# Batch 1's queries transposed by DMA, three parameter rows spread by TensorE, and batch 1's values loaded between the halves of W2

## The chip, the cores and the metric

One NeuronCore of a Trainium2 chip runs the whole kernel. Its engines are TensorE (PE, matrix products into PSUM; PEld is its loading of weights), VectorE (DVE), ScalarE (ACT) and GpSimd (POOL); SyncE (SP) and POOL issue the DMAs used here. SP's go to a hardware queue and POOL's to a software queue, which also converts types on the way. The metric is the device time of one execution in microseconds, from the first instruction to the end of the program, as a median of several runs.

## The reference

Four batches go through sorted attention and then through a residual MLP. Cut to what matters:

```python
for _ in range(5):                         # sort_net -> P, rows and columns normalised
    P = softmax-like row and column scaling
k_sorted = einsum('bhij,bhjcd->bhicd', P, k_blocks)   # 8 blocks of 96 positions
v_sorted = einsum('bhij,bhjcd->bhicd', P, v_blocks)
attn = softmax(q_block @ k_sorted_block.T / sqrt(64)) # block by block
x = (attn @ v_sorted_block)                           # -> [4, 768, 512]

a1 = alpha1 * x + beta1
u = x + lam * einsum('ts,bsd->btd', w_tok, a1)
a2 = alpha2 * u + beta2
out = u + lam * (relu(a2 @ w_ch1) @ w_ch2)            # 512 -> 2048 -> 512
```

q, k and v are [4, 8 heads, 768, 64], all inputs float32; the output is [4, 768, 512] float32. The kernel computes in float16 and bfloat16 with float32 sums.

## The kernel before

**Stages.** Batch 0's attention comes first, while weights load. Then TensorE goes through the batches in halves of 384 positions. For each batch b and half hf there is an "h" stage of 16 units (`h_unit`, lines 770 and 1088: 512 to 2048 with a ReLU on ACT) and a "c" stage, the product with W2. For batch 0 the c stage has three tiles of 128 positions (`ch_unit`, line 773), each in four parts, and after each part a slot "c", 0 to 11. Later batches use `ch_pair` instead.

**An order written out by hand.** Every engine works through its own list in program order; an instruction that waits holds back all behind it on that engine, and this goes for SP's and POOL's DMA issues too. `put(b, hf, kind, n, f)` (line 993) hangs a piece of work behind unit n of a stage, and `run` emits it there. So the attention of batch 1 is spread over the stages (0,0) and (0,1) of batch 0, and so on.

**Batch 1's attention.** It needs, in this order:

- k and v in `raw` tiles (`load_kv`, line 195, two POOL DMAs each) and q in `qn` (`load_q`, line 185). For batch 1 q comes in contiguous slabs (`load_slabs`), for later batches in position order, six POOL DMAs. The tag "qn" has one buffer, the tag "raw" two.
- `mix_v` (line 552): TensorE mixes the blocks of v by the sorting matrix, ACT copies the result to `mixed`; three parts. `bounce_v` writes `mixed` to DRAM in two DMAs and `back_v` (line 593) reads it back into `Vs` with positions on partitions, on SP, in one DMA.
- `mix_k` (line 567): three parts; TensorE mixes and turns the keys, ACT writes `kT` in four copies per part.
- q turned to `qT`. For batch 1, `q_turn_late` (line 538) does this four times by 24 small TensorE products with an identity and two VectorE copies; for later batches `q_cross` (line 531) does it with a transposing DMA on SP for each 128 positions.
- `score` (line 414): TensorE, then ACT's exponential; the first is at (0,1,"h",0), the next at 1 and 2. One score covers two heads and half of the positions, that is 384 columns of `qT`. `pv` (line 490) uses `Vs` from unit 3 on.

**Other work on the same queues.** `moe_cross(0, 1)` (line 732) turns u of batch 0's second half with three transposing DMAs on SP into `uT`, from which VectorE makes `a2T`, the input of stage (0,1) "h". The finished tiles `ost` are stored by SP (line 788). `loads(2)` (line 545), at slot c 11, has POOL copy one element of `Vs` first, so that the loads of batch 2 start when `Vs` is back.

**Parameters.** alpha1, beta1 and lam are loaded spread over 128 partitions by three POOL DMAs (lines 947 to 949) into `alphaB`, `betaB` (float16) and `lamB`. `scale_affine` (line 630) multiplies the first two by 64 lam on VectorE between the `first_finish` steps of batch 0, and `scale_weights` (line 793) makes `lam16` from `lamB` and scales W2p with it. `brow` holds beta1 * lam in single rows.

**Loads on POOL's queue**, in order: q, v, k of batch 0, w_tok, the three parameters, W1 in four pieces, W2 in four pieces, v, k and q of batch 1.

**PSUM.** Tag psA has two tiles of two banks each (`psa`), psB four tiles of one bank (`psb`). A tile's next user waits until the last one's reader is through.

Of the kernel before, what the change touches and what calls it, by code (L numbers as in the profile page):

```python
# [7 lines left out]
FT = mybir.dt.float32  # L8
F16 = mybir.dt.float16
BF = mybir.dt.bfloat16  # L10
AF = mybir.ActivationFunctionType
# [5 lines left out]
def kernel(  # L17
# [75 lines left out]
    def const(shape, dtype, name):  # L93
        return wts.tile(shape, dtype, name=name, tag=name)
# [11 lines left out]
    bet1 = att.tile([1, C], FT, name="bet1", tag="ost", bufs=4)  # L106
    nc.sync.dma_start(lam1[:], moe_lam.rearrange("(o c) -> o c", o=1))
    nc.sync.dma_start(bet1[:], moe_beta1.rearrange("(o c) -> o c", o=1))

    KT0 = att.tile([128, H4, NB, 128], F16, name="kT0", tag="tw", bufs=2)  # L110
    VD = att.tile([128, D, 64], F16, name="vd", tag="tw", bufs=2)
# [5 lines left out]
    def load_slabs(dst, src):  # L117
        flat = src.rearrange("h s d -> (h s d)").rearrange("(g p f) -> p g f", p=128, f=12 * D)
        for g in range(0, H4, 2):
            pool.dma_start(dst[:, g:g + 2, :], flat[:, g:g + 2, :])  # L120
# [54 lines left out]
    W2p = const([128, HT, C], F16, "W2p")  # L175
    w1v = moe_w_ch1.rearrange("(ci p) n -> p ci n", p=128)
    w2v = moe_w_ch2.rearrange("(m p) c -> p m c", p=128)
    alphaB = const([128, C], F16, "alphaB")
    betaB = const([128, C], F16, "betaB")
    lamB = att.tile([128, C], FT, name="lamB", tag="kT", bufs=1)  # L180
    vscr = dram.tile([B, H * NB, BLK, D], F16, name="vscr", tag="vscr")
    raw_of = {}
    qn_of = {}

    def load_q(b):
        if b == 1:
            qn_of[b] = att.tile([128, H4, 12 * D], F16, name="q8b", tag="qn", bufs=1)
            return load_slabs(qn_of[b], q[b])
        qn_of[b] = att.tile([128, NT, H, D], F16, name="qn", tag="qn", bufs=1)
        for kt in range(NT):  # L190
            pool.dma_start(
                qn_of[b][:, kt, :, :], q[b, :, kt * 128:(kt + 1) * 128, :].rearrange("h p d -> p h d"),
            )

    def load_kv(b):
        for kv, src in ((1, v), (0, k)):
            raw = att.tile([128, HB, D], F16, name="raw", tag="raw", bufs=2)
            load_halves(raw, src[b])
            raw_of[(b, kv)] = raw
# [38 lines left out]
    def turn_slab(src, rhs, g, name, ps):  # L238
        if ps is psa:
            ps = ps([128, 2, 512], FT, name)  # L240
            ps = [ps[:, a, 0:384] for a in range(2)]
        else:
            ps = [ps([128, 384], FT, name)[:] for a in range(2)]
        for s in range(12):
            for h2 in range(2):
                t = (s + 6 * h2) % 12
                r = slice(h2 * 64, h2 * 64 + 64)
                pe.matmul(
                    ps[t // 6][r, (t % 6) * 64:(t % 6) * 64 + 64],
                    src[r, g, t * D:(t + 1) * D], rhs(r, g), start=True, stop=True,  # L250
                )
        return ps

    def q_turn(b, g, ps):
        if g == 0:
            qT_of[b] = att.tile([128, H4, S], F16, name="qT", tag="qT", bufs=1)
        return turn_slab(qn_of[1] if b else q8, lambda r, g: ident16[r, r], g, "q_ps", ps)

    def q_copy(b, g, ps, half, eng):
        eng(  # L260
            qT_of[b][:, g, :].rearrange("p (r t) -> p r t", t=12)[:, :, half * 6:half * 6 + 6],
            ps[half].rearrange("p (t r) -> p r t", t=6),
        )
# [271 lines left out]
            qT_of[b][:, :, kt * 128:(kt + 1) * 128], qn_of[b][:, kt, :, :].rearrange("p h d -> p (h d)"),  # L535
        )

    def q_turn_late(g):
        ps = q_turn(1, g, psb)
        q_copy(1, g, ps, 0, dve.tensor_copy)  # L540
        q_copy(1, g, ps, 1, dve.tensor_copy)

    gate = const([1, 1], F16, "gate")

    def loads(b):
# [45 lines left out]
            )  # L591

    def back_v(b):
        sp.dma_start(Vs[0:BLK, :, 0:D], vscr[b].rearrange("x t d -> t x d"))

    w_tokT = const([128, NT, S], F16, "w_tokT")
    wp_of = {}
# [29 lines left out]

    GAIN = 64.0

    def scale_affine(t_):  # L630
        dve.scalar_tensor_tensor(t_[:], lamB[:], GAIN, t_[:], op0=ALU.mult, op1=ALU.mult)

    u_of = {}
    u16_of = {}
# [158 lines left out]
    def scale_weights(g):  # L793
        if g == 0:
            lam16 = lam_of[0] = att.tile([128, C], F16, name="lam16", tag="ost", bufs=4)
            dve.tensor_scalar(lam16[:], lamB[:], GAIN, 0.0, op0=ALU.mult, op1=ALU.add)
        w = W2p[:, 4 * g:4 * g + 4, :]
        dve.tensor_tensor(w, w, lam_of[0][:].unsqueeze(1).to_broadcast([128, 4, C]), ALU.mult)

# [144 lines left out]
    pool.tensor_tensor(brow[0:1, :], bet1[:], lam1[:], ALU.mult)  # L944
    for j in range(1, 4):
        sp.dma_start(brow[32 * j:32 * j + 1, :], brow[0:1, :])
    pool.dma_start(alphaB[:], moe_alpha1.partition_broadcast(128))
    pool.dma_start(betaB[:], moe_beta1.partition_broadcast(128))
    pool.dma_start(lamB[:], moe_lam.partition_broadcast(128))
    for g in range(2):  # L950
        pool.dma_start(W1p[:, :, g * 512:(g + 1) * 512], w1v[:, :, g * 512:(g + 1) * 512])
    permute(0, pool.tensor_copy, 0, 6)
    for g in range(2, 4):
        pool.dma_start(W1p[:, :, g * 512:(g + 1) * 512], w1v[:, :, g * 512:(g + 1) * 512])
    permute(1, pool.tensor_copy, 0, 6)
    for g in range(4):
        pool.dma_start(W2p[:, g * 4:(g + 1) * 4, :], w2v[:, g * 4:(g + 1) * 4, :])
    moe_start(0)
    a1_of[0] = moep.tile([128, 8, C], F16, name="a1", tag="a1", bufs=1)
    pv_first(0)  # L960
# [18 lines left out]
    first_turn(0, psb)  # L979
    pv_first(3)  # L980
    first_turn(1, psb)
    first_mm(2, psb)
    scale_affine(alphaB)
    first_turn(2, psa)
    scale_affine(betaB)

    load_kv(1)
    load_q(1)
    pool.memset(Vs[0:BLK, :, D:GRP], 1.0)

# [2 lines left out]
    def put(b, hf, kind, n, *todo):  # L993
        at.setdefault((b, hf, kind, n), []).extend(todo)
# [9 lines left out]
    put(0, 0, "h", 6, lambda: mix_matrix(1))  # L1004
    put(0, 1, "h", 1, lambda: mix_matrix(2))
    put(0, 1, "h", 2, lambda: mix_matrix(3))
    put(0, 0, "c", 0, lambda: moe_cross(0, 1))
    for g in range(CT):
        put(0, 0, "h", g, lambda g=g: first_affine(0, slice(0, 128), slice(0, NT), slice(g * 128, (g + 1) * 128)))
    for m in range(3):  # L1010
# [3 lines left out]
    for b in range(1, B):  # L1014
        p = b - 1
        if b == 1:
            for n in range(3):
                put(0, 0, "h", 13 + n, lambda n=n: mix_v(1, n, act.copy))
                put(0, 0, "c", 3 + 3 * n, lambda n=n: mix_k(1, n, (act.copy,) * 4))
            put(0, 0, "h", 15, lambda: bounce_v(1))  # L1020
            put(0, 0, "c", 2, lambda: back_v(1))
            for g in range(H4):
                put(0, 0, "c", (4, 5, 7, 8)[g], lambda g=g: q_turn_late(g))
            put(0, 0, "c", 11, lambda: loads(2))
            seq = [("s", 0), ("s", 1), ("s", 2), ("p", 0), ("s", 3), ("p", 1), ("p", 2), ("s", 4), ("p", 3), ("s", 5),
                   ("p", 4), ("s", 6), ("p", 5), ("s", 7), ("p", 6), ("p", 7)]
            for at_, (kind, n) in enumerate(seq):
                put(0, 1, "h", at_, (lambda n=n: score(1, n // 2, n % 2, psa)) if kind == "s" else (lambda n=n: pv(1, n // 2, n % 2)))
        else:
            for n in range(3):  # L1030
                put(p - 1, 1, "c", (n if b == 2 else 1 + n), lambda b=b, n=n: mix_v(b, n, act.copy))
            for n in range(3):
                put(p - 1, 1, "c", ((2, 5, 7), (4, 7, 10))[b - 2][n], lambda b=b, n=n: mix_k(b, n, (act.copy,) * 4))
            put(p - 1, 1, "c", b, lambda b=b: bounce_v(b))
            put(p - 1, 1, "c", (4 if b == 2 else 7), lambda b=b: back_v(b))
            for kt in range(NT):
                put(*((0, 1, "h", 13) if b == 2 else (1, 0, "c", 1)), lambda b=b, kt=kt: q_cross(b, kt))
            if b + 1 < B:
                put(p, 0, "h", 3, lambda b=b: loads(b + 1))
            for (kind, n), at_ in zip(  # L1040
                pairs, ((0, "h", 0), (0, "h", 2), (0, "h", 4), (0, "h", 6), (0, "h", 9), (0, "c", 0), (0, "c", 4), (1, "h", 2)),
            ):
                for i in range(2):
                    f = (lambda b=b, n=n + i: score(b, n // 2, n % 2, psa)) if kind == "s" else (lambda b=b, n=n + i: pv(b, n // 2, n % 2))
                    put(p, *at_, f)
            for at_ in ((0, "h", 5), (0, "h", 6), (0, "h", 10), (0, "h", 11), (1, "h", 0), (1, "h", 1), (1, "h", 3), (1, "h", 4)):
                put(p, *at_, flush_one)
        if b == 1:
            put(p, 1, "h", 15, flush)
        put(p, 1, "h", 3, lambda b=b: moe_start(b))  # L1050
        for kt in range(3):
            put(p, 1, *(("c", 3) if b == 1 else ("h", 9 + 2 * kt)), lambda b=b, kt=kt: moe_tok(b, kt, psb))
        put(p, 1, *(("c", 3) if b == 1 else ("h", 13)), lambda b=b: moe_cross(b, 0))
        for ci in range(CT):
            put(p, 1, "c", 8 if b == 1 else 8 + ci, lambda b=b, ci=ci: moe_affine(b, 0, (ci,)))
        for kt in range(3):
            put(b, 0, "h", 2 * kt, lambda b=b, kt=kt: moe_tok(b, 3 + kt, psb))
        put(b, 0, "h", 4, lambda b=b: moe_cross(b, 1))
        put(b, 0, "c", 2, lambda b=b: moe_affine(b, 1))
# [73 lines left out]
```

## Time and profile before

| what | us |
|---|---|
| median of three runs | 259.93 (259.82 to 260.39) |
| profiled execution | 259.8 |
| its span, first to last instruction | 257.9 |
| TensorE busy | 244.8 |
| ScalarE busy | 155.6 |
| VectorE busy | 173.5 |
| batch 0's first c stage on TensorE | 53.27 to 71.27 |
| first score of batch 1 | 72.01 |

The profiled execution took 259.8 us, 1.9 more than its span, because what lies ahead of the first and behind the last instruction counts as well. In the page, row 1 gives each engine's busy time, and row 2 cuts the span into 40 slices of 6.4 us: a digit is a tenth of busy share, PEclk is the clock that TensorE was granted, DMA the busy share of the 16 DMA engines. In a timeline a row is start, duration, engine, operation, output and inputs, shape and count; the bracket gives the idle time ahead of it and what ended that. A row with several instructions lasts from the first one's start to the last one's end, and since matmuls overlap, the difference of two starts tells more than a row's duration. In the list of DMA issues the columns are destination and source, queue, kind, count, KB of each, and the median time from issue to landing.

### The profile page before, as it was taken

The page shows a single profiled execution, that of the slowest core. Times are in us where ns is not written, and L with a number is a line of the kernel's source. Part 1 is how long each engine was busy: PE and PEld are TensorE (multiplying, and loading weights), DVE is VectorE, ACT ScalarE, POOL GpSimd, SP SyncE. Part 2 cuts the span into 40 slices and gives each one's busy share as a digit, 9 for nine tenths or more (in the row PEclk, how much of TensorE's full clock was granted, in tenths as well). Part 3 has the DMA queues.
Part 4 walks back from the last instruction along what each step waited for, and adds up shares of the span by engine and source line. Part 5 has one row for each costly group of instructions (what it writes and reads, how often), then busy time and mean ns, then how long its engine had stood idle before and what let it go on. Part 6 is the DMA issues. An engine that isn't in the chain of part 4 may idle for free.

```text
span 257.9 us, 6054 instructions
## 1 busy us (share of the span) xinstructions
PE 244.8 (95%) x2416; PEld 159.5 (62%) x2416; DVE 173.5 (67%) x461; ACT 155.6 (60%) x285; POOL 46.0 (18%) x70
## 2 busy tenths in 40 slices
PE   6897899999799999999999999999999999999994
PEld 2476564545456545456865787557756875686783
DVE  5886487764457969359896775298886873461873
ACT  4797475567197797687655587877465004847400
POOL 8699604000091010074000010000000000000000
PEclk9999999999799999999999999999999999999999
DMA  5999999999989976989992259910302232111023
GB/s 98 202 209 190 206 206 211 213 191 149 177 154 193 127 142 148 140 180 196 139 132 73 43 138 142 171 23 0 84 0 42 64 98 68 20 40 44 0 84 81
DMA packets 61936, 31.09 MB, mean 121 GB/s; under 512 B 50562, under 2 KB 57618, under 8 KB 61908
## 3 DMA queue, kind: packets, MB, share of 16 engines
q0 software_dynamic: 20976, 16.91, 45.1%
q1 hardware_dynamic: 40836, 13.76, 31.1%
q8 instruction: 19, 0.31, 0.5%
q14 instruction: 9, 0.07, 0.1%
q10 hardware_dynamic: 96, 0.03, 0.1%
HBM read 32.79 MB, written 8.65 MB: 161 GB/s over the span
## 4 chain that ended last, share of the span: by engine, by line
PE 77%; ACT 7%; DVE 6%; DMA 4%; issue 2%; POOL 1%; SPq 1%; DVEq 0%; ACTq 0%; POOLq 0%
PE h_ps L65 30%; PE tok_ps L65 11%; PE px L65 8%; PE ch_ps L65 6%; PE pz L65 6%; PE py L65 6%; DMA v<-in_v_dram 3%; PE x_ps L65 2%; PE sc_ps L65 2%; ACT et L65 2%; PE kmix_ps L65 2%; PE mix_ps L65 2%; DVE a2T L65 1%; ACT kT L65 1%; DVE ost L65 1%
## 5 line engine op out<-in xcount | busy, mean ns | idle before, releaser
L65 PE MATMUL h_ps<-a2T,W1p 128*128 128x384 bf16 x512 | 93.4, 326 | 0.3 <-DVE a2T L65 0.3
L65 PEld LDWEIGHTS <-W1p 128*128 128x128 bf16 x512 | 47.8, 98 | 30.7
L65 ACT ACTIVATE hTa<-h_ps 128x384 f16<-128x384 f32 x64 | 31.1, 489 | 30.4 <-PE h_ps L65 29.2
L65 ACT ACTIVATE hTb<-h_ps 128x384 f16<-128x384 f32 x64 | 31.3, 489 | 8.7 <-PE h_ps L65 8.7
L65 DVE SCALAR_TENSOR_TENSOR u<-tok_ps,x 128x512 f32<-128x512 f32 x21 | 14.5, 691 | 27.1 <-PE tok_ps L65 27.1
L65 ACT CAST kT<-kmix_ps 64x512 f16<-64x512 f32 x36 | 25.7, 713 | 10.8 <-PE kmix_ps L65 10.3
L65 PE MATMUL tok_ps<-a,w_tokT 128*128 128x512 f16 x126 | 30.3, 379 | 0.0
L65 ACT ACTIVATE et<-sc_ps 96x768 f16<-96x768 f32 (+2 forms) x36 | 24.5, 743 | 1.7 <-PE sc_ps L65 1.7
L65 ACT CAST u<-u 128x512 f16<-128x512 f32 x21 | 13.0, 618 | 20.5 <-DVE u L65 20.4
L65 PEld LDWEIGHTS <-sums 128*128 128x128 f16 x216 | 21.1, 98 | 3.5 <-issue 0.4
L65 PEld LDWEIGHTS <-hTa 128*128 128x128 f16 x192 | 18.4, 99 | 7.0 <-issue 0.5
L65 PEld LDWEIGHTS <-hTb 128*128 128x128 f16 x200 | 18.6, 98 | 6.2 <-issue 0.2
L65 PEld LDWEIGHTS <-w_tokT 128*128 128x128 f16 x126 | 12.3, 98 | 13.1 <-DVE a L65 0.3
L65 DVE TENSOR_TENSOR x<-x_ps,rcb 96x512 f16<-96x512 f32 x24 | 16.5, 687 | 0.8
L65 DVE TENSOR_TENSOR sums<-hTa,hTb 128x512 f16<-128x512 f16 (+2 forms) x27 | 8.9, 329 | 10.3 <-ACT hTb L65 10.0
L65 PEld LDWEIGHTS <-et 96*128 96x128 f16 (+4 forms) x288 | 12.0, 100 | 3.7 <-issue 1.1
L65 DVE SCALAR_TENSOR_TENSOR ost<-px,u 128x256 f32<-128x256 f32 x27 | 11.3, 418 | 3.4 <-PE px L65 3.4
L65 PE MATMUL x_ps<-Vs,et 96*128 96x65 f16 (+4 forms) x288 | 12.8, 195 | 0.8 <-issue 0.8
L65 PE MATMUL ch_ps<-W2p,hTa 128*128 128x512 f16 x48 | 12.7, 400 | 0.0
L65 PE MATMUL ch_ps<-W2p,hTb 128*128 128x512 f16 x48 | 11.8, 382 | 0.0
L65 POOL DMA_DIRECT2D qn<-in_q_dram x12 | 10.7, 924 | 3.4 <-DMA raw<-in_v_dram 2.9
L65 ACT CAST mixed<-mix_ps 128x1024 f16<-128x1024 f32 x9 | 9.2, 1017 | 3.6 <-PE mix_ps L65 3.6
(140 smaller groups left out, 351.9 us busy)
## 6 DMA issues: line engine op xcount, KB each, us to landing
out_dram<-ost SPq DMA_DIRECT2D x23, 192.0 KB, 2.4
raw<-in_v_dram POOLq DMA_DIRECT2D x6, 384.0 KB, 7.4
raw<-in_k_dram POOLq DMA_DIRECT2D x6, 384.0 KB, 10.3
Vs<-vscr SPq DMA_DIRECT2D x3, 768.0 KB, 7.7
W1p<-in_moe_w_ch_dram POOLq DMA_DIRECT2D x4, 512.0 KB, 11.6
W2p<-in_moe_w_ch_dram POOLq DMA_DIRECT2D x4, 512.0 KB, 15.6
qn<-in_q_dram POOLq DMA_DIRECT2D x12, 128.0 KB, 10.7
vscr<-mixed POOLq DMA_DIRECT2D x4, 384.0 KB, 5.1
```

The source lines that it names most:

```text
L65: ins = getattr(self.eng, name)(*args, **kwargs)
```

## The change

- **q of batch 1.** `load_q(1)` no longer loads slabs; q comes in position order in six POOL DMAs, and `q_cross(1, kt)` turns it with six transposing DMAs on SP, three at slot c 3 and three at c 5. `q_turn_late` goes.
- **v of batch 1.** Its two loads stand between the second and the third piece of W2. `mix_v(1, n)` moves from h 13, 14, 15 to h 11, 12, 13, `bounce_v(1)` from h 15 to h 13.
- **Vs of batch 1.** `back_v(1)` moves from SP at c 2 to POOL at c 0 and is cut into eight DMAs, one for each head.
- **Others.** `moe_cross(0, 1)` moves from c 0 to h 14, behind the bounce as before. `mix_k(1, n)` moves from c 3, 6, 9 to c 2, 5, 8.
- **Parameter rows.** The three broadcast loads go. SP loads alpha1 as one row; ACT makes 64 lam as a float32 and a float16 row, POOL multiplies the alpha1 and the beta1 row with it. `spread` has TensorE multiply a column of ones with a row of 512 (two rows for `affB`, one for `lam16`), and ACT copies the result to all partitions. `scale_affine` goes.

```diff
+    al1 = att.tile([1, C], FT, name="al1", tag="ost", bufs=4)
+    nc.sync.dma_start(al1[:], moe_alpha1.rearrange("(o c) -> o c", o=1))
...
-    alphaB = const([128, C], F16, "alphaB")
-    betaB = const([128, C], F16, "betaB")
-    lamB = att.tile([128, C], FT, name="lamB", tag="kT", bufs=1)
+    affB = const([128, 2, C], F16, "affB")
+    alphaB, betaB = affB[:, 0, :], affB[:, 1, :]
+    lam64 = att.tile([1, 3, C], FT, name="lam64", tag="kT", bufs=1)
+    rows = lam64[:].bitcast(F16)
+    arow, b64, lrow = rows[:, 1, 0:C], rows[:, 1, C:2 * C], rows[:, 2, 0:C]
...
     def load_q(b):
-        if b == 1:
-            qn_of[b] = att.tile([128, H4, 12 * D], F16, name="q8b", tag="qn", bufs=1)
-            return load_slabs(qn_of[b], q[b])
...
-    def load_kv(b):
-        for kv, src in ((1, v), (0, k)):
+    def load_kv(b, *kvs):
+        for kv in kvs or (1, 0):
+            src = (k, v)[kv]
...
-    def q_turn_late(g):
-        ps = q_turn(1, g, psb)
-        q_copy(1, g, ps, 0, dve.tensor_copy)
-        q_copy(1, g, ps, 1, dve.tensor_copy)
...
     def back_v(b):
-        sp.dma_start(Vs[0:BLK, :, 0:D], vscr[b].rearrange("x t d -> t x d"))
+        if b > 1:
+            return sp.dma_start(Vs[0:BLK, :, 0:D], vscr[b].rearrange("x t d -> t x d"))
+        for h in range(H):
+            x = slice(h * NB, (h + 1) * NB)
+            pool.dma_start(Vs[0:BLK, x, 0:D], vscr[b, x].rearrange("x t d -> t x d"))
...
-    def scale_affine(t_):
-        dve.scalar_tensor_tensor(t_[:], lamB[:], GAIN, t_[:], op0=ALU.mult, op1=ALU.mult)
+    def spread(dst, *srcs):
+        ps = psa([128, 2, 512], FT, "row_ps")
+        for a, src in enumerate(srcs):
+            pe.matmul(ps[:, a, :], ones[0:1, 0:1].to_broadcast([1, 128]), src, start=True, stop=True)
+        act.copy(dst, ps[:, 0:len(srcs), :])
...
-            dve.tensor_scalar(lam16[:], lamB[:], GAIN, 0.0, op0=ALU.mult, op1=ALU.add)
+            spread(lam16[:].unsqueeze(1), lrow)
...
-    pool.dma_start(alphaB[:], moe_alpha1.partition_broadcast(128))
-    pool.dma_start(betaB[:], moe_beta1.partition_broadcast(128))
-    pool.dma_start(lamB[:], moe_lam.partition_broadcast(128))
+    act.activation(lam64[:, 0, :], lam1[:], AF.Copy, scale=GAIN)
+    act.activation(lrow, lam1[:], AF.Copy, scale=GAIN)
...
-    for g in range(4):
+    def load_w2(g):
         pool.dma_start(W2p[:, g * 4:(g + 1) * 4, :], w2v[:, g * 4:(g + 1) * 4, :])
+
+    load_w2(0)
+    pool.tensor_tensor(arow, al1[:], lam64[:, 0, :], ALU.mult)
+    pool.tensor_tensor(b64, bet1[:], lam64[:, 0, :], ALU.mult)
+    load_w2(1)
+    load_kv(1, 1)
+    load_w2(2)
+    load_w2(3)
...
     first_turn(1, psb)
+    spread(affB[:], arow, b64)
     first_mm(2, psb)
-    scale_affine(alphaB)
     first_turn(2, psa)
-    scale_affine(betaB)
-
-    load_kv(1)
+
+    load_kv(1, 0)
     load_q(1)
...
-    put(0, 0, "c", 0, lambda: moe_cross(0, 1))
+    put(0, 0, "h", 14, lambda: moe_cross(0, 1))
...
-                put(0, 0, "h", 13 + n, lambda n=n: mix_v(1, n, act.copy))
-                put(0, 0, "c", 3 + 3 * n, lambda n=n: mix_k(1, n, (act.copy,) * 4))
-            put(0, 0, "h", 15, lambda: bounce_v(1))
-            put(0, 0, "c", 2, lambda: back_v(1))
-            for g in range(H4):
-                put(0, 0, "c", (4, 5, 7, 8)[g], lambda g=g: q_turn_late(g))
+                put(0, 0, "h", 11 + n, lambda n=n: mix_v(1, n, act.copy))
+                put(0, 0, "c", 2 + 3 * n, lambda n=n: mix_k(1, n, (act.copy,) * 4))
+            put(0, 0, "h", 13, lambda: bounce_v(1))
+            put(0, 0, "c", 0, lambda: back_v(1))
+            for kt in range(NT):
+                put(0, 0, "c", 3 + 2 * (kt // 3), lambda kt=kt: q_cross(1, kt))
```

More of the change, by code (lines that the diff above doesn't have):

```diff
@@ L256, in q_turn @@
             qT_of[b] = att.tile([128, H4, S], F16, name="qT", tag="qT", bufs=1)
-        return turn_slab(qn_of[1] if b else q8, lambda r, g: ident16[r, r], g, "q_ps", ps)
+        return turn_slab(q8, lambda r, g: ident16[r, r], g, "q_ps", ps)
     def q_copy(b, g, ps, half, eng):
```

## The prediction

> **What bounds the kernel now.** I read the page first, then the chain of waits, TensorE's timeline where the change sits, and the DMA issues.
>
> ```profile
> span 257.9 us, 6054 instructions
> ...
> PE 244.8 (95%) x2416; PEld 159.5 (62%) x2416; DVE 173.5 (67%) x461; ACT 155.6 (60%) x285; POOL 46.0 (18%) x70
> ...
> PEclk9999999999799999999999999999999999999999
> DMA  5999999999989976989992259910302232111023
> ```
>
> TensorE works 95% of the span and the chain is 77% PE, so the kernel ends when TensorE's list ends; from 72.7 us to the end the waits view shows TensorE no hole over 0.4 us. What counts is the one place with holes, slice 11 (the 7 in the clock row), where the DMA engines are still full too. TensorE there:
>
> ```profile
> 62.87 1.04 PE L65 MATMUL ch_ps<-W2p,hTa 128*128 128x512 f16 x4
> 65.70 0.19 PE L65 MATMUL q_ps<-ident,q8b 64*64 64x64 f16 x1 [1.80 <-DVE ost L65]
> 66.17 0.76 PE L65 MATMUL q_ps<-ident,q8b 64*64 64x64 f16 x23 [0.28 <-DVE qT L65]
> 66.86 1.89 PE L65 MATMUL ch_ps<-W2p,hTa 128*128 128x512 f16 x4
> ...
> 71.27 0.81 PE L65 MATMUL h_ps<-a2T,W1p 128*128 128x384 bf16 x4
> ...
> 73.72 0.34 PE L65 MATMUL sc_ps<-qT,kT 64*128 64x96 f16 x8
> ```
>
> The last turn of q waits 1.80 us for a bank: VectorE stands before ost until uT lands at 63.67 (chain: 60.67 3.00 DMA uT). Then the clock halves (0.51 in the window 66.2 to 69.7): four ch matmuls take 1.68 us start to start, not 0.86. Row 73.72 is score(1,0,1), the second score of batch 1; I measure the change there, because from there TensorE is dense.
>
> **Removed.** The late turns of q: 4 x 0.50 us (62.37 to 62.87) = 2.0; the wait 1.80 + 0.28; the slow clock (q 0.70 for 0.50, ch 1.68 for 0.86, kmix 0.85 for 0.44) 1.4. Sum 5.5 us of the stage 53.27 to 71.27, which by its rows needs 48 ch x 0.216 + 3 kmix x 0.44 = 11.7. VectorE loses eight casts (4.1 us). So the channel stage could end near 66.
>
> **Spread rows.** Three broadcast loads go: the load before them landed at 22.3 (9.2 + 13.1), the last of them at 26.0 (17.7 + 8.3), so the POOL queue runs 3.7 us ahead. Two VectorE multiplications (0.60 each, at 33.5 and 34.7) go. Added: three 512-wide matmuls (0.22 each by ch), an ACT copy of 1024 columns (1.02 by mixed) ahead of group 2's tok and z, another of about 0.6 for lam16, two ACT rows of about 0.55 each in ACT's hole at 20.5 (1.07), and two POOL products of 1.26 each while its queue has a backlog of over 10 us. The ACT copy delays z of group 2 by 0.7, and the last first_mm waits for its bank: 0.5 us to TensorE. Bounds: -0.4 (the holes in 33 to 41.5) to +1.0. It is covered if the stage's end is set by the transfers below; uncovered it counts in full.
>
> **Loads.** Before, W2 ended at 46.4 (27.9 + 18.5), v at 50.0, k at 53.7, q at 57.4. With 3.7 us less: v 41.3, W2 46.5 (3.8 us behind v), k 50.0. k can still not be issued before 40.65, since its buffer is wp's; the backlog hides that. q now goes as six loads of 64-element pieces: batch 2's six took 6.2 us (82.1 to 88.3), the two slabs 3.7. So q ends at 56.2, 1.2 earlier. W2 is first scaled at 49.1: no cost.
>
> **Bounce and SP's order.**
>
> ```profile
> 54.95 1.13 SPq L65 DMA_DIRECT2D vscr<-mixed  x2
> 56.26 6.03 SPq L65 DMA_TRANSPOSE uT<-u  x3
> 62.40 0.52 SPq L65 DMA_DIRECT2D Vs<-vscr  x1
> ```
>
> The mixes come two slots earlier; with the 0.5 us and ACT's copies the last ends at about 53.8 (54.93 before). The bounce moves after the queue drains, 1.1 earlier: landed about 61.1 (62.2), uT issued by 61.15 and landed by 62.6. moe_cross stays behind the bounce on SP, so its move earns no more. VectorE's a2T then ends near 63.9, ahead of the h stage, and no bank hangs on it.
>
> Behind uT on SP wait two output stores (0.9) and then six transposes of q, each 1.25 to 1.30 (batch 2: 7.77 for six): issued from 62.1 to 69.7. Behind these, the stores of two ch tiles, which nobody needs soon.
>
> **back_v on POOL.** Eight DMAs of 768 pieces: 0.83 each, between W1p's 0.75 (512 rows) and qn's 0.92 (1024), from 61.2 to 67.9. Then POOL comes to loads(2): gate (now released by head 0 alone), v and k of batch 2, issued 68.5 to 70.6, 1.9 us of transfer each. The old gate held these until all of Vs was back.
>
> **What a transfer of SP costs beside a POOL backlog** decides.
>
> ```profile
> raw<-in_k_dram POOLq DMA_DIRECT2D x6, 384.0 KB, 10.3
> Vs<-vscr SPq DMA_DIRECT2D x3, 768.0 KB, 7.7
> ...
> qT<-qn SPq DMA_TRANSPOSE x12, 3.0
> ...
> brow<-brow SPq DMA_DIRECT2D x3, 1.0 KB, 5.2
> ...
> P<-in_sort_net_dram SPq DMA_DIRECT2D x1, 8.0 KB, 1.5
> ```
>
> brow, 1 KB, took 5.2 us behind a POOL backlog that landed at 22.3; P, 8 KB, 1.5 on an idle chip. The transpose uT issued at 114.29 behind batch 3's loads landed 10.0 us later, against 2.4 for one without load. So I serve all DMAs in the order of issue. Work from 62.5: stores 1.3 (256 KB at some 200 GB/s); eight back_v at 0.65 (qn moved 4838 packets from 82 to 86, 1200 per us); six transposes at 0.6 (some 540 packets each, 2440 from 88.4 to 94: 0.45 at that rate, 1.25 by their issue, and I take a value near the first); loads 1.9 each (k's two halves landed 1.9 apart); landing 1.2 later (2.4 less the issue). Five back_v stand before the third transpose: it lands near 70.1. The last lands at 62.5 + 1.3 + 5.2 + 3.6 + 1.2 = 73.8 with no load ahead, 75.7 with one, 77.6 with two, 81.4 with four. The last is issued at 69.7, the first two loads at 69.0 and 69.5: one or two ahead; I take one, as SP may be half a microsecond early.
>
> The Trainium skill (DMA: Bandwidth & Descriptors, "Queues, rings and completion order") has each DMA engine take turns between the queues packet by packet, so a small transfer would slip past a backlog; brow's 5.2 us speaks against it. By that rule the sum would end near the first rival's, below. The same page's "Rules for kernel authors" counts overhead as most of a transfer under 64 KB and says to coalesce, which speaks against cutting back_v in eight; at 96 KB each, with qn's 128 KB landing 1 us apart, I add nothing for it.
>
> **Sum.** score(1,0,0) needs the first three transposes, score(1,0,1) all. TensorE ends ch at 66, does one h unit, waits to 70.1 and again to 75.7. score(1,0,1) at 75.8 for 73.72: +2.1. Bounds by the same rows: +0.2 with no load ahead, +7.8 with four. Two idle stretches drop the clock as at 66.27, where it came back after one full busy window of 3.4 us at half speed: +1.7. The execution with its 257.9 us span took 259.8 (1.9 lie around it): 259.8 + 2.1 + 1.7 = 263.6; that is 0.1 below the median of 259.93, so 263.7.
>
> **Rivals.**
> (a) Transposes slip past the loads: each goes as soon as it is issued, the last landing at 69.7 + 2.5 = 72.2; score at 72.3, -1.4, clock +1.0 to +1.7: 259.5 to 260.2, no change. For: queues share engines. Against: brow, uT. 0.12.
> (b) Faster: SP is free early. uT's first transpose took 3.05 us of SP instead of 1.2; if that stall goes with the earlier cross, SP starts q at 59.7 and ends at 67.2, ahead of all loads of batch 2; the last lands at 70.5 (67.2, 2.5, and 0.8 of the pieces beside it): score at 70.6, -3.1, clock +0.7 (less than half of a window): 257.5. Without any wait at all, -5.5 + 0.5: 254.9. The stall stands directly behind the two bounces, which stay there, so I hold it less likely. 0.26.
> (c) Worse: SP is held longer and all four loads go ahead: +7.8 + 1.7, 269.4. For: transposes issued in a backlog took SP up to 1.8 us instead of 1.2 (129.15). Against: by the sum at most three stand in the queue at once. 0.12.
> (d) W2's second half behind v comes late and the scaling waits: decides from 49.1; I have 46.5, 2.6 us of cover; each microsecond beyond costs one. Inside the others.
> Forecast, 261.7 (no load ahead) to 265.6 (two): 0.50.
>
> **How the numbers follow.** Slower: forecast and (c), 0.62. Same, within 0.2% (0.52 us, about what measurement tells apart): (a) less its edges, 0.10. Faster: (b) and an edge of (a), 0.28. Range 256.8 to 268.5: it leaves out the no-wait case (0.06) and most of (c); the forecast's own range is 261.7 to 265.6.
>
> **What shows it.** Right: no q_ps after 50 us, no halved clock near 66; sc_ps of batch 1 with idle before it, released by a DMA qT<-qn; its transposes landing over 5 us after issue; PEclk low around 70 to 80. Wrong: score(1,0,1) before 73, or transposes landing within 3 us beside back_v. The removed loads show as W1p landing near 24.8 for the first.

## The result, and the profile after

The changed kernel took 270.3 us (median of four runs, 269.92 to 272.49) against 260.1 for the kernel before on the same chip: a ratio of 1.041, with a 95% interval of 1.035 to 1.047. It is slower by 10 us. Where the executions of a kernel fall into a fast and a slow group, the times below are those of the fast one. The profiled execution has a span of 268.5 us for 257.9. The page of the changed kernel begins so (the same rows of the kernel before stand in the prediction):

```profile
span 268.5 us, 5888 instructions
...
PE 246.0 (92%) x2323; PEld 158.3 (59%) x2323; DVE 168.5 (63%) x450; ACT 158.5 (59%) x289; POOL 57.0 (21%) x81
...
PEclk9999999999755999999999999999999999999999
DMA  6999999999999927799996107950111133102022
```

TensorE is busy for about as long as before, but in a span that is 10.6 us longer. The clock row has one dip to 7 in the kernel before; now it reads 7, 5, 5, three slices of 6.7 us each. TensorE's timeline there, for the first two scores of batch 1:

```profile
63.80 1.89 PE L65 MATMUL ch_ps<-W2p,hTb 128*128 128x512 f16 x8
65.53 1.06 PE L65 MATMUL h_ps<-a2T,W1p 128*128 128x384 bf16 x4
68.66 0.22 PE L65 MATMUL sc_ps<-qT,kT 64*128 64x96 f16 x2 [2.07 <-DMA qT<-qn]
71.59 0.26 PE L65 MATMUL sc_ps<-qT,kT 64*128 64x96 f16 x2 [2.71 <-DMA qT<-qn]
73.09 0.34 PE L65 MATMUL sc_ps<-qT,kT 64*128 64x96 f16 x4 [1.24 <-DMA qT<-qn]
73.36 1.46 PE L65 MATMUL h_ps<-a2T,W1p 128*128 128x384 bf16 x4
81.16 0.94 PE L65 MATMUL sc_ps<-qT,kT 64*128 64x96 f16 x8 [6.17 <-DMA qT<-qn]
82.03 1.46 PE L65 MATMUL h_ps<-a2T,W1p 128*128 128x384 bf16 x4
```

The channel stage does end early: the first row of the h stage is at 65.53, where it was at 71.27. Then TensorE has four holes, 12.2 us in all, each ended by a transpose of q, and the second score stands at 81.16 instead of 73.72, which is 7.4 late. The h units around it take 1.46 us each for 0.82: half speed, from 70.8 to 87.8. The next c stage begins 17.0 us after the second score (98.20), before the change 13.9 (87.59). So the loss is 7.4 us by which the holes put off the second score and 3.2 us of slow clock behind it, together the 10.6 of the span.

What SP and POOL did at that time, in their own timelines (start, duration of the whole group, engine, operation, how many):

```profile
53.98 1.13 SPq L65 DMA_DIRECT2D vscr<-mixed  x2
55.30 6.27 SPq L65 DMA_TRANSPOSE uT<-u  x3
61.61 1.05 SPq L65 DMA_DIRECT2D out_dram<-ost  x2
62.71 14.52 SPq L65 DMA_TRANSPOSE qT<-qn  x6
77.31 2.14 SPq L65 DMA_DIRECT2D out_dram<-ost  x4
```

```profile
60.43 6.18 POOL L65 DMA_DIRECT2D Vs<-vscr  x8 [12.57 <-DMA vscr<-mixed]
66.60 0.18 POOL L65 COPY gate<-Vs 1x1 f16<-1x1 f16 x1
66.73 1.08 POOL L65 DMA_DIRECT2D raw<-in_v_dram  x2
67.78 1.19 POOL L65 DMA_DIRECT2D raw<-in_k_dram  x2
```

The six transposes begin to be issued at 62.71, 64.00, 65.34, 66.66, 68.00 and 69.47; the sixth then holds SP for 7.75 us, to 77.22. POOL issues all four loads of batch 2 between 66.73 and 68.97, before the sixth transpose begins. By the completion events in the trace those loads landed at 75.03, 76.94, 78.81 and 80.74, and the transposes at 68.52, 71.55 and 73.05, and then 81.11, 81.33 and 81.71. The fourth transpose was issued ahead of every load, and it landed behind them all. The DMA view, cut to two single microseconds, shows how:

```profile
DMA packets 96, 0.21 MB, mean 209 GB/s; under 512 B 64, under 2 KB 64, under 8 KB 96
...
q0 software_dynamic: 48, 0.20, 95.5%
q1 hardware_dynamic: 48, 0.01, 8.0%
...
DMA packets 64, 0.20 MB, mean 205 GB/s; under 512 B 32, under 2 KB 32, under 8 KB 64
...
q0 software_dynamic: 32, 0.20, 94.6%
q1 hardware_dynamic: 32, 0.01, 6.2%
```

The upper lines are the window 73 to 74, the lower ones 74 to 75; the columns are packets, MB and the share of the 16 DMA engines. In each the two queues moved exactly as many packets, 48 and 48, 32 and 32, and so it goes from 72 to 79: 272 and 272, with 1.38 MB for POOL's queue and 0.07 MB for SP's. The packets alternate, but a packet of a load holds some 5 KB and one of a transpose some 256 bytes. Beside the loads the transposes get a twentieth of the bytes; a transpose, over 500 packets long, then hardly moves until the loads are through. From 80 to 81, with nothing of POOL's queue beside them, SP's queue moved 970 packets.

### The profile page after: what moved, and what is told of

It reads as the page before. It is cut to its first block, busy times and chain, and to the rows that moved or that the text cites. A ratio compares the mean times of both kernels' runs of the same rounds, so it can differ in the third digit from the quotient of the medians.

```text
span 268.5 us, 5888 instructions
## 1 busy us (share of the span) xinstructions
PE 246.0 (92%) x2323; PEld 158.3 (59%) x2323; DVE 168.5 (63%) x450; ACT 158.5 (59%) x289; POOL 57.0 (21%) x81
## 4 chain that ended last, share of the span: by engine, by line
PE 74%; DMA 11%; ACT 7%; DVE 4%; POOL 2%; issue 1%; DVEq 0%; SPq 0%; POOLq 0%
PE h_ps L65 29%; PE tok_ps L65 11%; PE px L65 8%; PE pz L65 6%; PE py L65 5%; DMA qT<-qn 5%; PE ch_ps L65 4%; PE x_ps L65 3%; DMA q<-in_q_dram 3%; PE sc_ps L65 2%; POOL Vs L65 2%; DMA vscr<-mixed 2%; ACT et L65 2%; DMA Vs<-vscr 1%; PE mix_ps L65 1%
## 5 line engine op out<-in xcount | busy, mean ns | idle before, releaser
L65 PE MATMUL h_ps<-a2T,W1p 128*128 128x384 bf16 x512 | 96.0, 332 | 0.0
L65 PEld LDWEIGHTS <-W1p 128*128 128x128 bf16 x512 | 48.4, 99 | 32.6 <-issue 1.9
L65 ACT CAST u<-u 128x512 f16<-128x512 f32 x21 | 13.0, 618 | 20.4 <-DVE u L65 20.4
L65 PE MATMUL sc_ps<-qT,kT 64*128 64x96 f16 (+1 forms) x256 | 10.7, 211 | 13.5 <-DMA qT<-qn 12.2
L65 PEld LDWEIGHTS <-w_tokT 128*128 128x128 f16 x126 | 12.2, 98 | 13.1 <-DVE a L65 0.3
L65 POOL DMA_DIRECT2D qn<-in_q_dram x18 | 16.0, 910 | 14.1 <-DMA qT<-qn 13.3
L65 PEld LDWEIGHTS <-kT 64*128 64x128 f16 (+1 forms) x256 | 6.8, 97 | 20.5 <-issue 10.8
L65 PEld LDWEIGHTS <-et 96*128 96x128 f16 (+4 forms) x288 | 12.2, 101 | 3.0 <-issue 0.5
L65 POOL DMA_DIRECT2D vscr<-mixed x4 | 2.2, 558 | 48.1 <-ACT mixed L65 48.1
```

Source lines behind the costliest of these rows:

```text
L65: ins = getattr(self.eng, name)(*args, **kwargs)
```

## The experiments

Two theories were to be told apart at first: that the loads of batch 2 hold the transposes back (each at its transfer time), or that the transposes' own place on SP is what is late. All ratios are to the kernel before, timed on the same chip. Beside some of them stands the second score of batch 1 in the profiled execution, 73.72 in the kernel before. One such time is good to about 2 us: in the nine profiles with the same TensorE work up to there, the channel stage began between 53.03 and 55.41.

**The loads held back.** The gate that precedes the loads of batch 2 reads the last element of the turned q instead of Vs; in a second version the two loads of v go as before and only the loads of k wait.

```diff
     # no load ahead
-        pool.tensor_copy(gate[:], Vs[0:1, 0, 0:1])
+        pool.tensor_copy(gate[:], qT_of[1][0:1, H4 - 1, S - 1:S] if b == 2 else Vs[0:1, 0, 0:1])
         load_kv(b)
     # two loads ahead
         pool.tensor_copy(gate[:], Vs[0:1, 0, 0:1])
-        load_kv(b)
+        load_kv(b, 1)
+        if b == 2:
+            pool.tensor_copy(gate[:], qT_of[1][0:1, H4 - 1, S - 1:S])
+        load_kv(b, 0)
```

> The changed kernel, but the loads of batch 2 wait until the last transpose of batch 1's q has landed. Theory (the last three transposes wait for the four loads of v and k of batch 2 on POOL's queue, which were issued from 66.7 us on): nothing is ahead of them but back_v, so the last lands at 74 to 76 us instead of 81.7, the second score of batch 1 starts near 75 instead of 81.2, and the time is 262 to 265. Rival (the eight back_v DMAs and the transposes hold each other up, and the loads only stand behind): the last still lands at 79 or later and the time is 268 to 271.

> The changed kernel, but the two loads of k of batch 2 wait for the last transpose, while the two of v go as before. Theory: each load ahead costs its 1.9 us of transfer, so the last transpose lands 3.8 us later than with no load ahead, 78 to 80 us, and the time lies between that of no load and that of four, 265 to 268. Rival: as with the loads held back wholly, 268 to 271.

Measured: 263.06 us with no load ahead (1.014, 1.010 to 1.019) and 267.16 with two (1.032, 1.025 to 1.039). TensorE's timeline of the version with no load ahead:

```profile
70.50 0.22 PE L65 MATMUL sc_ps<-qT,kT 64*128 64x96 f16 x2 [2.58 <-DMA qT<-qn]
73.30 0.26 PE L65 MATMUL sc_ps<-qT,kT 64*128 64x96 f16 x2 [2.59 <-DMA qT<-qn]
74.33 0.34 PE L65 MATMUL sc_ps<-qT,kT 64*128 64x96 f16 x4 [0.76 <-DMA qT<-qn]
```

The hole of 6.17 us is gone. From the issue of the first transpose to the landing of the last it took 11.7 us with no load, 15.3 with two and 19.0 with four: 3.65 us for each pair, 1.8 a load, which is a load's own transfer time (they landed 1.9 apart). So the loads hold the transposes back by their whole length. But with none of them the second score is still at 76.16, 2.4 later than before the change, and 1.4% stay lost. Of these 2.4 us, 1.4 stand ahead of the channel stage, which began at 54.67 for 53.27. The rest was not taken apart by a run of its own. Six transposes with hardly anything of POOL's queue beside them take about as long: batch 2's in the kernel before 10.2 us (85.88 to 96.07), and 10.5 in the version below that issues them from 55.89 on. So sharing the DMA engines with the eight pieces of Vs can account for 1.2 to 1.5 us of the 11.7; most of it is the transposes' own time.

**The clock's share.** Idle TensorE products are put into the holes, so that it never rests long enough to be slowed; what is computed stays.

```diff
         for ii in range(4):
+            if b == 1 and g == 0:
+                warm(((9, 11, 5, 0), (30, 0, 0, 0))[hf][ii], psb)
             i = 4 * hf + ii
```

> The changed kernel with idle matmuls of 512 columns placed ahead of the first blocks of the first score (9, 11, 5) and ahead of the second score (30), so that TensorE works while it waits. Theory (the waits are the transfers', and the half clock from 70.8 to 87.9 us is a second loss of its own): the transposes land as before, the second score starts at 81 to 82.5, the clock stays at 1.0, and the six units of work after it no longer take double time: 2 to 3 us less, 267 to 268.5. Rival (the clock costs nothing beyond the waits): 270 to 271.5.

Measured 268.30 (1.036, 1.033 to 1.040). The granted clock was 1.0 throughout, the second score at 81.25, as late as without the products. The next c stage came 13.9 us behind that score (95.13), as in the kernel before: the whole 3.2 us of slow clock were taken back there. The span fell by only 2.0, since the h stage then had a new wait of 0.59 us for a2T at 112.77. The clock is a consequence; the holes are the cause.

**q turned by TensorE again.** All else of the change stays: v early, Vs on POOL, the rows spread.

```diff
     def load_q(b):
+        if b == 1:
+            qn_of[b] = att.tile([128, H4, 12 * D], F16, name="q8b", tag="qn", bufs=1)
+            return load_slabs(qn_of[b], q[b])
...
-            for kt in range(NT):
-                put(0, 0, "c", 3 + 2 * (kt // 3), lambda kt=kt: q_cross(1, kt))
+            for g in range(H4):
+                put(0, 0, "c", (4, 5, 7, 8)[g], lambda g=g: q_turn_late(g))
```

> The changed kernel with q of batch 1 loaded in slabs and turned by TensorE as before the change (all else as changed: rows spread by PE, v early, back_v on POOL, mixes earlier). Theory (only the transposes of q lose time): no score of batch 1 waits for a DMA; the channel stage is as before the change, 2 us of turns and a wait for uT that lands near 64: 258.5 to 261.5. Rival (spread rows, back_v on POOL or the earlier mixes lose time as well): 263 or more.

Measured 257.95 (0.994, 0.990 to 0.998), faster than the kernel before, and the second score at 72.90. So the transposes are the whole loss, and the rest of the change is worth half a per cent. (q's loads change with them, but in the changed kernel they had landed at 55.28, 7 us ahead of the first transpose of q.) One hole is left, the old one, smaller:

```profile
67.45 0.19 PE L65 MATMUL q_ps<-ident,q8b 64*64 64x64 f16 x1 [0.96 <-DVE ost L65]
67.92 0.54 PE L65 MATMUL q_ps<-ident,q8b 64*64 64x64 f16 x23 [0.28 <-DVE qT L65]
```

**The transposes earlier on SP.** If their place is what counts, they should go ahead of the loads. In the first version SP issues u's transposes, then q's, then the bounce of v, all at h 13; in the second q's go first, at h 12.

```diff
-    put(0, 0, "h", 14, lambda: moe_cross(0, 1))
...
-            put(0, 0, "h", 13, lambda: bounce_v(1))
+            put(0, 0, "h", 13, lambda: moe_cross(0, 1))
+            for kt in range(NT):
+                put(0, 0, "h", 13, lambda kt=kt: q_cross(1, kt))
+            put(0, 0, "h", 13, lambda: bounce_v(1))
...
-            for kt in range(NT):
-                put(0, 0, "c", 3 + 2 * (kt // 3), lambda kt=kt: q_cross(1, kt))
```

> The changed kernel with another order on SP: uT's three transposes and q's six are issued before the bounce of v (all at h 13) and no longer after the stores of c 3. Theory (what loses time is that q's transposes stand behind back_v and the loads of batch 2; early enough, they move while nothing else is queued): they land by 64, the first two scores of batch 1 wait for no DMA, the second starts at 67 to 69 instead of 73.7 before the change and 81.2 after it; the bounce is 6 to 8 us later and the first pv may wait 1 to 2 us for Vs; 253 to 257. Rival (the transposes are slow wherever they stand, as DMAs of many small packets): q lands at 70 or later and the time is 259 or more.

> As the run before it in this list, but q's transposes ahead of uT's (h 12), then uT and the bounce at h 13. Theory: q lands by 60, uT by 63, so VectorE has uT just before the h stage, and Vs comes 2 us earlier than there; 253 to 257. Rival: uT now lands after 65.5 and TensorE waits for it, 257 to 260.

Measured 263.46 (1.011, 1.007 to 1.015) and 262.55 (1.009, 1.006 to 1.012): better than the change, but both expectations of 253 to 257 were wrong. The scores no longer wait (second score at 68.31 and 68.87). But the bounce now stands behind nine transposes on SP and is issued at 65.20 and 64.88 instead of 53.98, so Vs is late, and the first product with it waits. TensorE's timeline of the two:

```profile
74.88 0.21 PE L65 MATMUL x_ps<-Vs,et 96*128 96x65 f16 x1 [4.31 <-DMA Vs<-vscr]
```

```profile
74.24 0.19 PE L65 MATMUL x_ps<-Vs,et 96*128 96x65 f16 x1 [3.11 <-DMA Vs<-vscr]
```

The hole moved from q to Vs. In none of the three orders tried do nine transposes and the bounce fit on SP in the time between the mixes and the scores. A bounce on POOL, as batch 2 has it, was not tried.

**Vs in one DMA on SP.** As before the change, in place of eight on POOL, so that POOL's queue should be empty while the transposes are issued.

```diff
     def back_v(b):
-        if b > 1:
+        if b > 0:
             return sp.dma_start(Vs[0:BLK, :, 0:D], vscr[b].rearrange("x t d -> t x d"))
...
-            put(0, 0, "c", 0, lambda: back_v(1))
+            put(0, 0, "c", 2, lambda: back_v(1))
```

> The changed kernel with back_v of batch 1 as one DMA on SP at c 2, as it was before the change, so that the loads of batch 2 wait again until all of Vs is back. Theory: the loads start 2 to 3 us later and only one or two of them get ahead of the last transposes; the second score starts at 75 to 78, 263 to 267. Rival (back_v on POOL in eight pieces is itself the loss): the second score at 73 to 74, 258 to 261.

Measured 270.94 (1.043, 1.038 to 1.048), no better than the change, and again outside what was expected. SP's timeline:

```profile
60.84 0.52 SPq L65 DMA_DIRECT2D Vs<-vscr  x1
61.41 5.45 SPq L65 DMA_DIRECT2D out_dram<-ost  x2
66.91 11.26 SPq L65 DMA_TRANSPOSE qT<-qn  x6
```

The store behind the long transfer of Vs holds SP until 66.4, so the transposes start 4.2 us later than in the change and meet the same loads (issued 69.47 to 71.70).

**The spread of the rows alone**, on the kernel before:

> The kernel before, with only the parameter rows spread by TensorE instead of loaded 128-fold. Prediction's term: 0.5 us more on TensorE ahead of the channel stage (bounds -0.4 to +1.0), while all loads of POOL's queue land 3.7 us earlier and so uT and the channel stage's stall 1 to 2 us earlier: 257.5 to 260. Rival (the spread's ACT copy and matmuls cost more than the queue gains): 260.5 or more.

Measured 261.26 (1.004, 1.001 to 1.008): a small loss where a small gain was expected. It is so near the noise that the profiled execution, at 259.78, does not show it in its time. The edit is the parameter part of the diff above and nothing else. TensorE's timeline ahead of the first h stage, of this version and of the kernel before (`row_ps` is the product in `spread`):

```profile
31.48 0.34 PE L65 MATMUL turn_ps<-ident,x 128*128 128x128 f16 x3
31.91 0.60 PE L65 MATMUL row_ps<-lam,ones 1*128 1x512 f16 x2
32.45 1.15 PE L65 MATMUL tok_ps<-w_tokT,x 128*128 128x384 f16 x6
...
33.97 0.65 PE L65 MATMUL h_ps<-a2T,W1p 128*128 128x384 bf16 x3
```

```profile
31.24 0.34 PE L65 MATMUL turn_ps<-ident,x 128*128 128x128 f16 x3
31.58 1.14 PE L65 MATMUL tok_ps<-w_tokT,x 128*128 128x384 f16 x6
...
32.89 0.49 PE L65 MATMUL h_ps<-a2T,W1p 128*128 128x384 bf16 x2
```

From this turn to the first h unit it is 2.49 us, and 1.65 in the kernel before. Of the 0.84 more, 0.63 lie between the turn and `tok_ps`, where the two wide products stand, and 0.21 behind it, where ScalarE copies their result. All ten profiles with the spread rows show these 2.5 us, all three without them 1.65. From the first h unit to the channel stage it is 20.4 us either way, so the third product costs next to nothing.

The two rows of 64 lam on ScalarE can cost something too. They take 1.13 us in a hole that is 1.07 long in the kernel before, and in this profile TensorE's `k_ps` waits 1.47 us for them, where it waited 1.03 for the exponentials before. Such a wait for lam, of 1.2 to 1.7 us, stands in five of the ten profiles. In return the time from the channel stage to the second score is shorter, 19.3 us for 20.5, so that the second score comes at 73.70, as before.

**Only VectorE's order.** In the kernel before the last turn of q waits because VectorE stands before u's transposes (a2T at slot c 6). One line moves that work behind the casts of q:

```diff
-    put(0, 0, "c", 6, lambda: moe_affine(0, 1))
...
+            put(0, 0, "c", 9, lambda: moe_affine(0, 1))
             put(0, 0, "c", 11, lambda: loads(2))
```

The same line was moved in the version with q turned by TensorE (best1), and from that the spread of the rows was taken out again (best2).

> The kernel before with one line moved: VectorE's a2T of batch 0's second half from slot c 6 to c 9, behind the casts of the last q turn. If the 1.80 + 0.28 us hole of TensorE at the last q turn is only VectorE standing before uT's landing, it goes, and the halved clock behind it (1.4) with it: 256.5 to 258 (ratio 0.987 to 0.993), second score near 71. If the hole only moves to the h stage (a2T late) or the time is bound elsewhere: 259.5 to 260.5.

> The changed kernel with q's slabs and TensorE turns (as in qpe) and a2T at slot c 9. qpe had 0.96 + 0.28 us left at the last turn; without them 256.5 to 257.5 (ratio 0.986 to 0.991), second score near 71.7. If the turn's hole has another cause than a2T's place: 257.9 as qpe.

> best1 with the parameter rows loaded spread again, as before the change. In the experiment rows the spread alone lost 0.4 per cent (0.2 to 0.7 per cent), 1 us; if that holds here, 255.5 to 256.8, below best1. If the three spared loads are what lets v come early enough, best2 is slower than best1: 257.5 to 259.

Measured: 257.55 for the one line alone (0.990, 0.987 to 0.993), 256.37 for best1 (0.985, 0.981 to 0.988) and 255.57 for best2 (0.982, 0.979 to 0.985). best2 is the fastest version of this study, 4.7 us below the 260.23 of the kernel before in the same runs. Its page and its TensorE timeline:

```profile
span 253.4 us, 6062 instructions
...
PEclk9999999999999999999999999999999999999998
```

```profile
67.74 0.34 PE L65 MATMUL sc_ps<-qT,kT 64*128 64x96 f16 x8
68.90 0.34 PE L65 MATMUL sc_ps<-qT,kT 64*128 64x96 f16 x8
```

No hole, no slow clock, the second score 4.8 earlier than before. best1 and best2 differ by 0.8 us, about what the rows lost by themselves, though their intervals overlap; from the channel stage to the second score both take 16.0 us, so the difference lies ahead of it. The one line alone gave back some of its gain further on, as its TensorE timeline shows:

```profile
102.55 1.19 PE L65 MATMUL h_ps<-a2T,W1p 128*128 128x384 bf16 x4 [1.00 <-DVE a2T L65]
```

best2 has no such wait. What sets it was not tried.

## Why the prediction was right and wrong

The direction and the place were right: the channel stage loses its hole, and the scores then wait for transposes of q that stand beside POOL's transfers. The number of loads that they wait for was wrong, and so was the rule that it came from. The time was 6.6 us above the forecast of 263.7 and above the range of 256.8 to 268.5.

- **Channel stage near 66, no q_ps behind 50, no slow clock at 66.** As forecast: it ends at 65.53, 11.7 us after its start, as its rows had it.
- **Rows, +0.5.** The place was right, the products and the ACT copy behind them. The size was 0.84, inside the bounds of -0.4 to +1.0. The two ACT rows do not always fit into the hole that I had put them into. That the channel stage began at 53.83 for 53.27 shows nothing, since it moves by 2 us from profile to profile.
- **POOL's queue 3.7 earlier.** The first W1p landed at 24.85 (24.8), v at 41.87 (41.3), W2 at 46.47 (46.5), k at 50.78 (50.0), q at 55.28 (56.2). W2's cover held; rival (d) did not happen.
- **Bounce and SP.** The bounce was issued at 53.98 (53.8) but landed at 59.82, 1.3 earlier than forecast. The transposes were issued when I had them, 62.71 to 69.47 for 62.1 to 69.7.
- **back_v and the loads.** Eight DMAs at 0.77 each from 60.43, for 0.83 from 61.2: together 1.3 us earlier at the end. The gate behind them took 0.1 us instead of 0.6, so that the loads went out from 66.73 to 68.97 instead of 68.5 to 70.6.
- **"One or two ahead; I take one".** This is the step that failed. All four were issued before the sixth transpose, the last landing was at 81.71, and the second score came 7.4 us later than before the change instead of 2.1. My own sum had 81.4 for four loads, and the price of 1.9 us a load was right (1.8 by the experiments). The count hung on half a microsecond on two queues, which I saw for SP and took as a reason for fewer. The rule behind the count was wrong too: I served the DMAs in the order of issue, and the fourth transpose, issued ahead of all the loads, landed behind them. The third, forecast for 70.1, landed at 73.05; this cost nothing only because the second score waits for the sixth. What counts is not how many loads are issued ahead but how many are issued before the transposes have moved their last packet, and by that rule all four were in it without any doubt: by the forecast's own times they were issued by 70.6, and the last transpose would land at 73.8 even with no load ahead.
- **Clock, +1.7.** Mis-sized: 3.2 us. I reckoned with one full window of 3.4 us at half speed behind the last hole. The clock stayed at half from 70.8 to 87.8, and 6.7 us of that lay behind the second score. The half-speed stretches that end inside a profile last 3.41, 6.83, 13.65, 17.07 or 20.48 us, all multiples of 3.41. On that grid the dense work began at 81.16, 0.1 us into a window that began at 81.02. TensorE was busy for 93% of that window and the clock did not come back at its end, only at the end of the next. In the profile of the rows alone it did come back behind a window busy for 93%, so why two windows were needed here stays open.
- **The sum by these terms:** 259.9 + 7.4 + 3.2 = 270.5, measured 270.3.

Rival (a), that transposes slip past the loads, is refuted. The Trainium skill (DMA: Bandwidth & Descriptors, "Queues, rings and completion order") has each engine switch between queues at every packet; I set it aside for the 5.2 us of brow, and read it as if it favoured the small transfer. What held brow, whose first packet moved only 3.9 us after its issue, stays open. The counts of 272 and 272 packets agree with the rule. What it favours is the queue with the larger packets: 5 KB against 256 bytes here.

Rival (b), the faster one, hung on the first transpose of u taking SP 3.05 us. It took 3.07 again. Where no bounce stood ahead of it, in the version with u's transposes first, it took 1.30 (issued 51.89, done 53.19). So the stall goes with the place behind the bounce, as I had held.

Rival (c) has the time (269.4) and the event, all four loads ahead. Its reason, that SP would be held longer, was not the one: SP was on time until 69.5, and POOL was early.

## What to carry to other kernels

When a transfer of many small packets runs beside another queue's large ones, count all that the other queue will be given before the small one is through, and charge it in full; moving the small ones ahead helps only if nothing else is pushed back on the same issuing engine. Before replacing work that an engine waits for, look at why it waits: here one line in VectorE's order gave 1%, and the transposes that were to remove the wait cost 4%. A hole in TensorE can cost more than its length, because the slow clock goes on through the work behind it: here 3.2 us on top of the 7.4.

## What the runs showed of the hardware beyond that

- **A transpose that can't get on holds its issuing engine.** Issue took 1.2 us each for the first four transposes of q, and 7.75 us for the sixth, until 77.22; from 72 on the queue moved 32 to 48 packets a microsecond. With two loads ahead the sixth took 3.92, with none 2.47. A plain store did the same behind the transfer of Vs on SP: 4.98 us for an issue that takes 0.4 to 0.6 in the changed kernel.
- **The slow clock is kept by intermittent work.** TensorE was busy 3.70 of the 16 us from 66 to 82, and the clock came back to 1.0 only at 87.85, 6.7 us after it had become dense.
- **Small waits early in the kernel may start it too.** Of the ten profiles with the spread rows, five show a window of 3.4 us at half speed between 14 and 27 us. Four of the windows begin between 22.3 and 23.4, and these are four of the five profiles in which `k_ps` waits for the rows of lam. Of the three profiles with broadcast rows none has such a window. With one profile of each version this is a hint, and it was not followed up.
